# Attention products of a chunk in one TensorE run with a drain, key transposes three chunks ahead, order keys set anew

## The chip, the cores and the metric

The kernel runs on one core of one Trainium2 chip. The metric is device time in microseconds of a whole execution. The kernel before takes 573.67 us, the median of three runs that lie between 573.64 and 573.75.

## The reference

An attention block with a decaying state (4 batches, 8 heads, 768 steps, head size 48) is followed by a feed-forward block over the 3072 tokens (384 in, 2048 hidden).

```python
for t in range(S):
    cur = np.einsum('bhd,bhe->bhde', u[None] * kt, vt)
    y[:, :, t] = np.einsum('bhd,bhde->bhe', rt, state + cur)
    state = wt[:, :, :, None] * state + np.einsum('bhd,bhe->bhde', kt, vt)
...
h = x @ w_in
g = h * np.clip(h + 3.0, 0.0, 6.0) / 6.0
return g @ w_out
```

## The kernel before

**Tiling.** The 768 steps of a batch are cut into chunks of 128, so there are 24 chunks, numbered 0 to 23; neighbouring numbers belong to two different batches, so that a chunk's state comes from the chunk two numbers before. A chunk is worked on as two halves of 64 steps. Eight heads lie as four pairs, one head of a pair on partitions 0 to 47, the other on 64 to 111. Four chunks make a block of 512 tokens, and the feed-forward part runs over six blocks. Block 0 uses plain products (`up`, L639; half of `down`, L658); every other product of the feed-forward part uses seven half-size products in place of eight (`up_product`, L740; `down_product`, L791). All matrices are fp32; on TensorE each matmul stands in the trace as two records.

**One chunk.** `back_scan` (L372, VectorE) runs over the decays from the end and gives E, `make_k` (L392) multiplies the keys with it, `fore_scan` (L381) and `make_r` (L396) do the same for the receptance. From chunk 7 on the two multiplications are GpSimd's. `own` and `own_dot` or `own_sum` give the diagonal of the score matrix, `diagonal` (L431, ScalarE) writes it into A with eight instructions, `above` (L447, VectorE) lays the upper triangle of the scores over it. TensorE has five parts: `score` (L440, 16 matmuls of 48 rows), `turn_k` (L456, four transposes of the keys over the full array), `write` (L536, up to 16 matmuls of 64 rows: keys times values, what the chunk adds to the state), `read_state` (L514, up to 16 matmuls of 48 rows: the state's share of the output) and `read_values` (L523, 16 matmuls of 64 rows: A times values). The last two add into the same PSUM tile y_ps from different rows of the array. `turned_k`, `written` and `leave` (ScalarE, L461, L543, L606) copy results out of PSUM.

**Two runs on TensorE.** From chunk 4 on, `begin(i)` issues `read_state(i)` and the transposes of chunk i+2; `read(i)`, later, issues `write(i+2)`, `read_values(i)` and `score(i+1)`. Feed-forward products stand between the two. For the last two chunks there is no `write`, and `read` issues a TensorE drain before `read_values` (L560). Chunks 0 to 3 use `read_last` and `read_rest` (L566 to L590), which have drains of their own and in which three chosen rows of a fourth pair go through an extra product (L584). Keys are transposed on their own (`turn`) up to chunk 5.

**Buffers.** K has two buffers, W (which becomes R) two, E, kn, kvs and the PSUM tiles y_ps and ps one each. The loads of a chunk's features (feat_in, 676 KB) share three buffers with 22 loads by which the kernel examines its inputs again (`refetch`, L820): a feature buffer comes free when the chunk's K and R (and `own` up to chunk 8) are made.

**Order.** `Plan` (L83 to L185) sets the order of all instructions when the program is built. Each step is added with an engine, an assumed duration, the steps that it needs, the rings of buffers that it holds and a key. The planner walks through an assumed time and, on the engine that can start first, takes the ready step with the lowest key. It emits matmuls of an identity on TensorE (`spin`, L1130) where it expects idle time before the first step of `up`. The keys come from the constants in L28 to L39: LAG and LEAD say how far ahead of its place in a block a chunk's `read` and `begin` are due, AHEAD when features are made, START the features of the first six chunks, CONV the conversion of the weights from 64-bit words (L331 to L359), UP the first block's up products, SUMS the sums of weights for the seven-product form (L687 to L712).

Of the kernel before, what the change touches and what calls it, by code (L numbers as in the profile page):

```python
# [23 lines left out]
BC = 4  # L24
GBC = 3


LAG = 6.1  # L28
AHEAD = -3.5
LEAD = 2.5  # L30
BEHIND = (-1, -1, -1, 0, 6, 7)
BY_PE = 9
OWN = 0.07
SOLO = (0, 2, 3, 4, 5)
EARLY = 7
START = (-118.3, -135.2, -24.4, -60.3, -5.9, 13.2)
CONV = (-100.6, 7.2)
UP = (-68.7, 1.2, -9.3, 6.3)
SUMS = (52.1, 1.4)  # L39
LEAST = 2.0 ** -60  # L40
# [147 lines left out]
def fast_path(tc, feat, tok, wflat, ub, ug, moe_w_in, moe_w_out, out, flag, n_chunks):  # L188
# [21 lines left out]
    with ExitStack() as ctx:  # L210
# [151 lines left out]

        for r, k in (("E", 1), ("K", 2), ("W", 2), ("rk", 1), ("dg", 2), ("A", 2), ("kn", 1), ("S", 2), ("x", 2), ("kvs", 1), ("y", 1),
                     ("ps", 1), ("bankA", 2), ("bankB", 1), ("bankC", 2), ("clip", 2), ("g0", 1), ("g1", 1), ("o", 2),
                     ("T_", 1), ("S_", 1)):
            plan.ring(r, k)
# [22 lines left out]
        def make_k(i):  # L389
            d = st[i]  # L390
            d["K"] = wk.tile([PR, 2 * P, HL], F32, name="K", bufs=2)
            early(i).tensor_mul(d["K"], d["k"], d["E"][:, :, 1:])  # L392
# [59 lines left out]
        def turn_k(i):  # L452
            d = st[i]
            d["kn_ps"] = pp.tile([L, P, PR], F32, name="ps")
            for p in range(P):
                nc.tensor.transpose(d["kn_ps"][:, p, :], d["K"][:, 2 * p:2 * p + 2, :].rearrange("q a t -> q (a t)"), ident[0:PR, 0:PR])  # L456
# [92 lines left out]

        def begin(i):  # L550
            new_y(i)
            read_state(i, range(P))
            if i + 2 < NT:
                turn_k(i + 2)

        def read(i):
            if i + 2 < NT:
                write(i + 2)
            else:
                nc.tensor.drain()  # L560
            read_values(i, range(P))
            if i + 1 < NT:
                score(i + 1)

# [323 lines left out]
        def turned_by(i):  # L888
            return f"turn{i}" if i <= BC + 1 else f"begin{i - 2}"

# [3 lines left out]
        for i in range(NT):  # L894
            t = when(i)
            k = START[i] if i < len(START) else when(i - 2) - AHEAD
            first, last = is_first(i), is_last(i)
            dve = i < EARLY
            behind = [f"fetch{BEHIND[i]}"] if i < len(BEHIND) and BEHIND[i] >= 0 else []
            plan.add(f"feat{i}", "SP", 0.45 if i else 1.15, do(load_feat, i), behind + [f"feat{i - 1}"] * (i > 0) + ["later"] * (i == 1), k - 20, kb=690 if i else 231,  # L900
                     hold=[("feat", [f"K{i}", f"R{i}"] + [f"own{i}"] * (i < BY_PE))])
# [13 lines left out]
            plan.add(f"least{i}", "ACT", 0.2, do(least, i), [f"back{i}"], k + 0.2)  # L915
            if i < BY_PE:
# [15 lines left out]
            plan.add(f"above{i}", "DVE", 0.76, do(above, i), [scored(i), f"diag1{i}"], due + 0.5)  # L932
            if i <= BC + 1:
                plan.add(f"turn{i}", "PE", 0.45, do(turn_k, i), [f"K{i}"] + [f"turn{i - 1}"] * (i > 0), due + 0.01, [("ps", [f"turned{i}"])])
            plan.add(f"turned{i}", "ACT", 0.53, do(turned_k, i), [turned_by(i)] + [f"turned{i - 1}"] * (i > 0), due - 2 if i > BC + 1 else due + 0.5,
                     [("kn", [written_by(i)])])
# [4 lines left out]
            S_ = [("S", [f"read{i}" if i < BC else f"begin{i}"] + [f"state{i}"] * (not last))]  # L941
            if not first:
# [13 lines left out]
            if bk == 0:  # L956
                plan.add(f"first{i}", "PE", 0.55 if first else 0.65, do(read_last, i), [f"above{i}", f"decb{i}"], t + 0.01, y)
                plan.add(f"third{i}", "ACT", 0.5, do(leave_last, i), [f"first{i}"], t + 0.01,
                         ([("x", all_up), ("S_", [f"read{j}" for j in range(BC)])] if i == 0 else []))
                plan.add(f"read{i}", "PE", 2.3 if first else 2.5, do(read_rest, i), [f"third{i}"] + [f"turned{i + 1}", f"tok{i + 1}"] * (i + 1 not in SOLO), t + 0.01)  # L960
                plan.add(f"leave{i}", "ACT", 1.0, do(leave_rest, i), [f"read{i}"], t + 0.02)
            else:
                uses = [f"up{bk}.{q}.{k_}" for q in range(HF) for k_ in (1, 2, 3, 4, 7)] + [f"tx{bk}.1"]
                space = [("x", uses)] * (c == 0)
                needs, us, banks = [f"begin{i}", f"above{i}"], 0.6, []
                if i + 2 < NT:
                    y.append(("ps", [f"turned{i + 2}"]))
                    needs += [f"turned{i + 2}", f"tok{i + 2}"]
                    us += 0.43
                if i + 1 < NT:  # L970
                    needs.append(f"R{i + 1}")
                    banks = [("bankB", [f"above{i + 1}"]), ("bankC", [f"above{i + 1}"])]
                    us += 0.49
                plan.add(f"begin{i}", "PE", 1.04 if i + 2 < NT else 0.6, do(begin, i), [f"decb{i}"] + [f"K{i + 2}"] * (i + 2 < NT),
                         t - LEAD, y)
                plan.add(f"read{i}", "PE", us, do(read, i), needs, t + 0.01, banks)
                plan.add(f"leave{i}", "ACT", 1.5, do(leave, i), [f"read{i}"], t + 0.5, space)
                if c % 2:
                    for g in range(2):
                        plan.add(f"move{bk}.{c // 2}.{g}", "SP", 1.8, do(last_pair, bk, c - 1, c + 1, g, nc.sync),  # L980
                                 [f"leave{i - 1}", f"leave{i}"], when(i) - 50, kb=1, dmas=3)
# [488 lines left out]
```

## Time and profile before

| | |
|---|---|
| median of three runs | 573.67 us (573.64 to 573.75) |
| span of the profiled execution | 570.5 us |
| outside the span, median less span | 3.2 us |
| TensorE matmul busy | 558.8 us, 98% |
| TensorE weight load busy | 501.8 us, 88% |
| VectorE busy | 405.2 us, 71% |
| ScalarE busy | 273.5 us, 48% |
| GpSimd busy | 100.3 us, 18% |
| mean granted TensorE clock | 0.992 |
| first `up` product starts | 32.32 us after the span's start |

The profile shows one execution, whose first and last instruction lie 570.5 us apart. No separate run time of that execution is given; the 3.2 us between its span and the median of the runs is taken as what lies around the span. A timeline row gives start and duration of a group of equal instructions; since matmuls overlap, the time that a group costs is the start of the next group less its own start. Idle time before an instruction stands in brackets with what ended it.

### The profile page before, as it was taken

How to read it: one execution, taken by the hardware profiler on the slowest of the kernel's cores; microseconds unless marked ns; L12 is line 12 of the kernel's file. 1: busy time of each engine (PE TensorE's matmuls, PEld its weight loads, DVE VectorE, ACT ScalarE, POOL GpSimd, SP SyncE). 2: the span in 40 equal slices, each digit the busy share in tenths (PEclk: the TensorE clock that was granted, in tenths of full speed). 3: DMA queues.
4: the chain of work that ended last, by engine and by line, in shares of the span. 5: the costliest groups of instructions: out<-in, count | busy, mean ns of one | idle time of the engine just before them, and what ended most of it. 6: DMA issues, size and time to landing. Idle time of an engine off the chain costs nothing.

```text
span 570.5 us, 13575 instructions
## 1 busy us (share of the span) xinstructions
PE 558.8 (98%) x5636; PEld 501.8 (88%) x5636; DVE 405.2 (71%) x713; ACT 273.5 (48%) x724; POOL 100.3 (18%) x111
## 2 busy tenths in 40 slices
PE   8999899999999999999999999999999999999996
PEld 8898587689888999988999988999988999988996
DVE  7989989988687858767879767879656625255350
ACT  4778664642565633276633366633266611355100
POOL 2000000245513321223123133123122000000000
PEclk9989899999999999999999999999999999999999
DMA  8977822531613236830368360366100001000001
GB/s 279 310 237 223 275 66 63 158 111 42 182 56 90 87 124 204 241 100 9 125 206 274 98 167 7 128 199 225 41 16 2 9 1 36 29 1 1 1 15 47
DMA packets 23078, 63.98 MB, mean 112 GB/s; under 512 B 3120, under 2 KB 10352, under 8 KB 23008
## 3 DMA queue, kind: packets, MB, share of 16 engines
q1 hardware_dynamic: 22880, 63.02, 36.0%
q8 instruction: 46, 0.75, 0.6%
q14 instruction: 24, 0.20, 0.1%
q10 hardware_dynamic: 128, 0.00, 0.0%
HBM read 57.31 MB, written 4.72 MB: 109 GB/s over the span
## 4 chain that ended last, share of the span: by engine, by line
PE 94%; DVE 2%; DMA 1%; ACT 1%; issue 1%; SPq 0%; DVEq 0%; ACTq 0%
PE bankA L791 20%; PE bankA L740 18%; PE bankC L791 10%; PE bankC L740 9%; PE bankB L740 6%; PE bankB L791 5%; PE bankC L639 3%; PE bankA L639 3%; PE bankA L658 3%; PE y_ps L514 3%; PE y_ps L523 2%; PE y_ps L536 2%; PE ps L456 2%; PE bankB L440 2%; DMA feat_in<-in_feat_dram 1%; PE bankA L1130 1%
## 5 line engine op out<-in xcount | busy, mean ns | idle before, releaser
L749 ACT COPY g<-bankA 128x256 f32<-128x256 f32 x120 | 44.3, 371 | 58.7 <-PE bankA L740 56.6
L791 PE MATMUL bankA<-w_out,g 128*128 128x192 f32 x352 | 63.9, 328 | 0.0
L629 ACT ACTIVATE clip<-g,three 128x512 f32<-128x512 f32 x80 | 57.9, 723 | 7.9 <-DVE g L751 7.2
L740 PE MATMUL bankA<-xT,w_in 128*128 128x256 f32 x240 | 60.2, 383 | 0.0
L791 PEld LDWEIGHTS bankA<-w_out,g 128*128 128x128 f32 x352 | 57.9, 190 | 0.9
L759 DVE SCALAR_TENSOR_TENSOR g<-clip,g 128x512 f32<-128x512 f32 x80 | 56.4, 707 | 2.8 <-ACT clip L629 2.6
L804 ACT ACTIVATE o<-bankA 128x192 f32<-128x192 f32 x33 | 10.9, 330 | 88.8 <-PE bankA L791 88.8
L740 PEld LDWEIGHTS bankA<-xT,w_in 128*128 128x128 f32 x240 | 44.8, 190 | 6.0
L431 ACT ACTIVATE A<-eyes,dg 128x64 f32<-128x64 f32 x192 | 49.2, 336 | 0.4
L606 ACT COPY xT<-y_ps 48x256 f32<-48x256 f32 x80 | 29.3, 366 | 37.3 <-PE y_ps L523 36.4
L392 POOL TENSOR_TENSOR K<-feat_in,E 112x512 f32<-112x512 f32 x17 | 21.5, 1266 | 136.6 <-PE bankC L440 121.6
L740 PE MATMUL bankB<-xT,w_in 128*128 128x256 f32 x160 | 41.1, 379 | 0.0
L751 DVE TENSOR_TENSOR g<-bankB,g 128x256 f32<-128x256 f32 x40 | 16.9, 423 | 32.4 <-PE bankB L740 30.7
L396 POOL TENSOR_TENSOR W<-feat_in,W 112x512 f32<-112x512 f32 x17 | 23.1, 1356 | 87.2 <-DVE W L381 87.2
L751 DVE TENSOR_TENSOR g<-bankC,g 128x256 f32<-128x256 f32 x40 | 16.8, 421 | 28.3 <-PE bankC L740 28.2
L740 PEld LDWEIGHTS bankB<-xT,w_in 128*128 128x128 f32 x160 | 30.4, 190 | 4.1
L381 DVE TENSOR_TENSOR_SCAN W<-feat_in,start 112x520 f32<-112x520 f32 x24 | 30.6, 1274 | 3.1 <-PE y_ps L514 3.0
L372 DVE TENSOR_TENSOR_SCAN E<-feat_in,back 112x520 f32<-112x520 f32 x24 | 30.0, 1250 | 2.5 <-DMA feat_in<-in_feat_dram 2.4
L791 PE MATMUL bankA<-bits,g 128*128 128x192 f32 x176 | 30.3, 328 | 0.4 <-DVE o L806 0.4
L791 PE MATMUL bankB<-w_out,g 128*128 128x192 f32 x176 | 30.4, 326 | 0.0
L791 PEld LDWEIGHTS bankA<-bits,g 128*128 128x128 f32 x176 | 28.8, 190 | 0.9 <-DVE o L806 0.7
L791 PEld LDWEIGHTS bankB<-w_out,g 128*128 128x128 f32 x176 | 28.9, 190 | 0.0
(277 smaller groups left out, 1213.8 us busy)
## 6 DMA issues: line engine op xcount, KB each, us to landing
feat_in<-in_feat_dram SPq DMA_DIRECT2D x23, 675.9 KB, 5.6
bits<-in_moe_w_in_dram SPq DMA_DIRECT2D x8, 768.0 KB, 9.6
bits<-in_moe_w_out_dram SPq DMA_DIRECT2D x8, 768.0 KB, 4.7
feat_in<-in_moe_w_in_dram SPq DMA_DIRECT2D x8, 768.0 KB, 4.3
feat_in<-in_moe_w_out_dram SPq DMA_DIRECT2D x8, 768.0 KB, 4.2
rk_in<-in_tok_dram SPq DMA_DIRECT2D x15, 384.0 KB, 5.9
v_in<-in_tok_dram SPq DMA_DIRECT2D x24, 192.0 KB, 4.0
out_dram<-o SPq DMA_DIRECT2D x24, 192.0 KB, 2.1
```

The lines of the kernel that those rows point to most:

```text
L372: nc.vector.tensor_tensor_scan(out=E_[:, ::-1], data0=d["w"][:, :0:-1], data1=back.rearrange("q p t -> q (p t)")[:, ::-1], initial=0.0, op ...
L381: nc.vector.tensor_tensor_scan(out=W_, data0=d["w"][:, :-1], data1=starts[i % 2].rearrange("q p t -> q (p t)"), initial=0.0, op0=ALU.mult, ...
L396: early(i).tensor_mul(d["R"], d["r"], d["R"])
L431: nc.scalar.activation(out=d["A"][:, h, :], in_=eyes, func=ACT.Copy, scale=d["dg"][:, h])
L606: nc.scalar.copy(out=blocks[bk]["xT"][g * GP:g * GP + D, :, at:at + HL], in_=st[i]["y_ps"][(g ^ a) * GP:(g ^ a) * GP + D, a, :, :])
L629: nc.scalar.activation(out=c[:, :m], in_=src, func=ACT.Relu, bias=three, scale=1.0)
L639: nc.tensor.matmul(h_ps[:, :(c1 - c0) * L], lhsT=w_in[:, f // 2, j, f % 2, :], rhs=b["xT"][:, j, c0 * L:c1 * L], start=(j == 0), stop=(j = ...
L740: nc.tensor.matmul(b["p", q, to][:, :HB], lhsT=w, rhs=rhs, start=(n == 0 and k in (1, 2, 5)), stop=(n == len(terms) - 1 and k in (2, 3, 4) ...
L749: nc.scalar.copy(out=to, in_=src)
L751: nc.vector.tensor_add(to, src, to)
L759: nc.vector.scalar_tensor_tensor(out=g, in0=b["r", q, p], scalar=6.0, in1=g, op0=ALU.min, op1=ALU.mult)
L791: nc.tensor.matmul(b["d", p, to][:, :h], lhsT=a, rhs=w(), start=(f == 0 and k in (1, 2, 5)), stop=(f == HF - 1 and k in (2, 3, 4)), skip_g ...
```

## The change

The two runs of a chunk become one. `begin` goes; `read(i)` now issues the transposes of chunk i+3, `read_state(i)`, `score(i+1)`, a drain, `write(i+2)` and `read_values(i)`. The transposes move from two chunks ahead to three, K gets a third buffer, transposes on their own go on to chunk 6, and the features for K (load, `back_scan`, `make_k`, `least`) get keys of their own that are earlier than those of `fore_scan` and `make_r`. The assumed durations of `read` and all keys are new. A parameter of the program's builder sets the scratch space of dynamic DMAs to 8192. What is computed is the same.

```diff
-LAG = 6.1
-AHEAD = -3.5
-LEAD = 2.5
+LAG = 21.433
+AHEAD = -20.818
+AHEAD_K = 3
+EARLIER = 35.468
...
-OWN = 0.07
+OWN = 0.713
...
-START = (-118.3, -135.2, -24.4, -60.3, -5.9, 13.2)
-CONV = (-100.6, 7.2)
-UP = (-68.7, 1.2, -9.3, 6.3)
-SUMS = (52.1, 1.4)
+START = (-107.75, -155.5, -31.0, -50.26, 12.19, 17.64)
+CONV = (-101.07, 9.16)
+UP = (-49.32, 1.47, -3.81, 4.04)
+SUMS = (139.7, -3.91)
...
-            d["K"] = wk.tile([PR, 2 * P, HL], F32, name="K", bufs=2)
+            d["K"] = wk.tile([PR, 2 * P, HL], F32, name="K", bufs=3)
...
-        def begin(i):
+        def read(i):
+            if i + AHEAD_K < NT:
+                turn_k(i + AHEAD_K)
             new_y(i)
             read_state(i, range(P))
-            if i + 2 < NT:
-                turn_k(i + 2)
-
-        def read(i):
+            if i + 1 < NT:
+                score(i + 1)
+            nc.tensor.drain()
             if i + 2 < NT:
                 write(i + 2)
-            else:
-                nc.tensor.drain()
             read_values(i, range(P))
-            if i + 1 < NT:
-                score(i + 1)
...
             k = START[i] if i < len(START) else when(i - 2) - AHEAD
+            kk = k if i < len(START) else when(max(BC, i - AHEAD_K)) - (EARLIER if i > BC + AHEAD_K else EARLIER + 2.0 * (BC + AHEAD_K - i))
...
-            plan.add(f"back{i}", "DVE", 1.4, do(back_scan, i), [f"feat{i}"] + [f"fore{i - 2}"] * (i > 1) + [f"back{i - 1}"] * (i > 0), k,
+            plan.add(f"back{i}", "DVE", 1.4, do(back_scan, i), [f"feat{i}"] + [f"fore{i - 2}"] * (i > 1) + [f"back{i - 1}"] * (i > 0), kk,
...
-                     k + 0.1, [("K", [scored(i), turned_by(i)])], port=True)
+                     kk + 0.1, [("K", [scored(i), turned_by(i)])], port=True)
...
-                     [("W", [scored(i), f"read{i}" if i < BC else f"begin{i}"])], port=True)
+                     [("W", [scored(i), f"read{i}"])], port=True)
...
-                needs, us, banks = [f"begin{i}", f"above{i}"], 0.6, []
+                needs, us, banks = [f"above{i}", f"decb{i}"], 1.15, []
+                if i + AHEAD_K < NT:
+                    y.append(("ps", [f"turned{i + AHEAD_K}"]))
+                    needs.append(f"K{i + AHEAD_K}")
+                    us += 0.4
                 if i + 2 < NT:
-                    y.append(("ps", [f"turned{i + 2}"]))
                     needs += [f"turned{i + 2}", f"tok{i + 2}"]
                     us += 0.43
                 if i + 1 < NT:
                     needs.append(f"R{i + 1}")
                     banks = [("bankB", [f"above{i + 1}"]), ("bankC", [f"above{i + 1}"])]
-                    us += 0.49
-                plan.add(f"begin{i}", "PE", 1.04 if i + 2 < NT else 0.6, do(begin, i), [f"decb{i}"] + [f"K{i + 2}"] * (i + 2 < NT),
-                         t - LEAD, y)
-                plan.add(f"read{i}", "PE", us, do(read, i), needs, t + 0.01, banks)
+                    us += 0.44
+                plan.add(f"read{i}", "PE", us, do(read, i), needs, t + 0.01, y + banks)
...
-    nc = _bacc.Bacc("TRN2", target_bir_lowering=False, num_devices=1)
+    nc = _bacc.Bacc("TRN2", target_bir_lowering=False, num_devices=1, dynamic_dma_scratch_size=8192)
```

In the built program the order of every engine is new. TensorE has the same matmuls apart from 49 identity matmuls instead of 53; the runs of small-array matmuls (`score`, `write`, `read_state`, `read_values`, several in one run if nothing else lies between) are 36 instead of 55.

More of the change, by code (lines that the diff above doesn't have):

```diff
@@ L360, in high_low @@
                                     in1=c["more"].bitcast(I32), op=ALU.add)
-        for r, k in (("E", 1), ("K", 2), ("W", 2), ("rk", 1), ("dg", 2), ("A", 2), ("kn", 1), ("S", 2), ("x", 2), ("kvs", 1), ("y", 1),
+        for r, k in (("E", 1), ("K", 3), ("W", 2), ("rk", 1), ("dg", 2), ("A", 2), ("kn", 1), ("S", 2), ("x", 2), ("kvs", 1), ("y", 1),
                      ("ps", 1), ("bankA", 2), ("bankB", 1), ("bankC", 2), ("clip", 2), ("g0", 1), ("g1", 1), ("o", 2),
@@ L888, in turned_by @@
         def turned_by(i):
-            return f"turn{i}" if i <= BC + 1 else f"begin{i - 2}"
+            return f"turn{i}" if i < BC + AHEAD_K else f"read{i - AHEAD_K}"
         def written_by(i):
@@ L899, in fast_path @@
             behind = [f"fetch{BEHIND[i]}"] if i < len(BEHIND) and BEHIND[i] >= 0 else []
-            plan.add(f"feat{i}", "SP", 0.45 if i else 1.15, do(load_feat, i), behind + [f"feat{i - 1}"] * (i > 0) + ["later"] * (i == 1), k - 20, kb=690 if i else 231,
+            plan.add(f"feat{i}", "SP", 0.45 if i else 1.15, do(load_feat, i), behind + [f"feat{i - 1}"] * (i > 0) + ["later"] * (i == 1), kk - 20, kb=690 if i else 231,
                      hold=[("feat", [f"K{i}", f"R{i}"] + [f"own{i}"] * (i < BY_PE))])
@@ L906, in fast_path @@
                          hold=[("rk_in", [f"own{i}"])])
[L907 removed]
+            plan.add(f"back{i}", "DVE", 1.4, do(back_scan, i), [f"feat{i}"] + [f"fore{i - 2}"] * (i > 1) + [f"back{i - 1}"] * (i > 0), kk,
                      [("E", [f"K{i}", f"least{i}"])], port=True)
             plan.add(f"K{i}", "DVE" if dve else "POOL", 0.66 if dve else 1.32, do(make_k, i), [f"back{i}", f"least{i}"] + [f"K{i - 1}"] * (i > 0) + ["later"] * (i == 0),
[L910 removed]
+                     kk + 0.1, [("K", [scored(i), turned_by(i)])], port=True)
             plan.add(f"fore{i}", "DVE", 1.23, do(fore_scan, i), [f"back{i}"] + [f"fore{i - 1}"] * (i > 0), k + 0.2,
[L912 removed]
+                     [("W", [scored(i), f"read{i}"])], port=True)
             plan.add(f"R{i}", "DVE" if dve else "POOL", 0.66 if dve else 1.32, do(make_r, i), [f"fore{i}"], k + 0.3,
                      port=True)
[L915 removed]
+            plan.add(f"least{i}", "ACT", 0.2, do(least, i), [f"back{i}"], kk + 0.2)
             if i < BY_PE:
@@ L932, in fast_path @@
             plan.add(f"above{i}", "DVE", 0.76, do(above, i), [scored(i), f"diag1{i}"], due + 0.5)
-            if i <= BC + 1:
+            if i < BC + AHEAD_K:
                 plan.add(f"turn{i}", "PE", 0.45, do(turn_k, i), [f"K{i}"] + [f"turn{i - 1}"] * (i > 0), due + 0.01, [("ps", [f"turned{i}"])])
-            plan.add(f"turned{i}", "ACT", 0.53, do(turned_k, i), [turned_by(i)] + [f"turned{i - 1}"] * (i > 0), due - 2 if i > BC + 1 else due + 0.5,
+            plan.add(f"turned{i}", "ACT", 0.53, do(turned_k, i), [turned_by(i)] + [f"turned{i - 1}"] * (i > 0), due - 2 if i >= BC + AHEAD_K else due + 0.5,
                      [("kn", [written_by(i)])])
@@ L940, in fast_path @@
                      [("kvs", [f"decb{i}"] if last else [f"state{i}"])])
-            S_ = [("S", [f"read{i}" if i < BC else f"begin{i}"] + [f"state{i}"] * (not last))]
+            S_ = [("S", [f"read{i}"] + [f"state{i}"] * (not last))]
             if not first:
```

## The prediction

> **What bounds the kernel now.** I read the page's busy line and its clock row, the chain that ended last, TensorE's own waits, then timelines around single chunks. The page first:
>
> ```profile
> PE 558.8 (98%) x5636; PEld 501.8 (88%) x5636; DVE 405.2 (71%) x713; ACT 273.5 (48%) x724; POOL 100.3 (18%) x111
> ...
> PEclk9989899999999999999999999999999999999999
> ...
> PE 94%; DVE 2%; DMA 1%; ACT 1%; issue 1%; SPq 0%; DVEq 0%; ACTq 0%
> ```
>
> TensorE (PE) is busy 98% and is 94% of the chain: time is saved only by issuing less on it, by switching its array less often, or where it stands still or runs at a lower clock. The list of waits, TensorE's alone, shows where it stands still; all of them lie before 151 us:
>
> ```profile
> PE y_ps L536 <- ACT kn L461: 1.6, 2, 0.9
> PE y_ps L584 <- ACT xT L576: 0.6, 1, 0.6
> PE bankB L440 <- DVE A L447: 0.5, 1, 0.5
> PE bankA L658 <- DVE w_out L359: 0.4, 1, 0.4
> ```
>
> The busy table by stretch shows two stretches with half the clock (column PEclk, after five pairs of busy time and count):
>
> ```profile
> 28.90:32.30 3.40, 3.40 (x24) 3.37 (x17) 3.37 (x6) 3.12 (x8) 0.00 (x0) 0.50 0.76 212
> 66.40:69.85 3.45, 3.34 (x17) 1.43 (x20) 3.28 (x4) 2.22 (x5) 0.00 (x0) 0.51 0.92 327
> ```
>
> Each costs 1.7 us (half of 3.4) where TensorE is what counts. The third thing is the switching. A steady chunk in the timeline, first `begin` (L514, L456), then `read` (L536 to L791):
>
> ```profile
> 281.07 1.47 PE L791 MATMUL bankA<-w_out,g 128*128 128x192 f32 x8
> 282.47 0.67 PE L514 MATMUL y_ps<-W,S 48*48 48x64 f32 x32
> 283.06 0.60 PE L456 MATMUL ps<-ident,K 112*128 112x112 f32 x4
> 283.50 1.48 PE L791 MATMUL bankA<-w_out,g 128*128 128x192 f32 x8
> 284.82 2.76 PE L791 MATMUL bankB<-w_out,g 128*128 128x192 f32 x16
> 287.42 1.46 PE L791 MATMUL bankA<-w_out,g 128*128 128x192 f32 x8
> 288.81 0.62 PE L536 MATMUL y_ps<-v_in,kn 64*64 64x48 f32 x30
> ...
> 290.33 1.57 PE L791 MATMUL bankC<-bits,S__3062 128*128 128x192 f32 x8
> 291.74 0.49 PE L791 MATMUL bankB<-w_out,g 128*128 128x192 f32 x2
> ```
>
> Eight L791 records take 1.30 us start to start in full flow (284.82 to 287.42 is 2.60 for 16). The eight ahead of L514 take 1.40 and those ahead of L536 1.39, so entering small tiles costs 0.095. The eight after `read` take 1.41: leaving costs 0.11 there, besides some 0.13 inside the 1.52 of `read` (288.81 to 290.33). `begin` is 0.10 + 0.59 + 0.44 + 0.02 (1.32 for the eight after it) = 1.15 us, `read` 0.09 + 1.52 + 0.11 = 1.72, a chunk 2.87.
>
> What a drain costs shows at chunk 22, which has no keys to turn and nothing to write:
>
> ```profile
> 454.12 0.67 PE L514 MATMUL y_ps<-W,S 48*48 48x64 f32 x32
> 454.90 0.67 PE L523 MATMUL y_ps<-A,v_in 64*48 64x64 f32 x32
> ```
>
> L514 and the gap take 0.78; L514's own starts span 0.45 (0.59 above less the 0.14 to the first transpose). The gap is 0.33, against some 0.03 between small matmuls without a drain.
>
> **What the Trainium skill says.** "TensorEngine Tiling (Array Packing)", section Key Properties, says that a change of tiling mode, not of the tile alone, drains TensorE. The trace agrees: 0.095 us going in and 0.24 coming out, but next to nothing between L536, L523 and L440, whose starts even interleave. "TensorE: Matmul & The Clock Gate", Part 1, says that the clock is halved after an idle window of about 3.4 us and that the windows run free of the kernel; here the two half-clock stretches last 3.41 us, both after stretches full of short matmuls, drains and waits. The same page, Part 3, has weight loads overlap running matmuls only where row groups differ; that a drain forbids even this fits the 0.33.
>
> **The change part by part.**
>
> *One run instead of two* (18 chunks, 4 to 21). Transposes between full-size products take 0.39 us (startup, L456 at 44.87, next product at 45.26). So the new run is: transposes 0.39 and 0.02, entry 0.095, L514 0.45, L440 with L536 and L523 and the way out 1.52 + 0.11, the drain 0.30 more than a plain step, and 0.03 because L440 now follows L514 and no longer slides into L523 (that overlap was -0.025, the step from L440 to L514 at 62.2 us is 0.038). Sum 2.92 against 2.87: +0.05 a chunk, +0.9 us in all. One entry and one exit go (0.095 + 0.24), a drain comes (0.30), and the transposes lose a place where they covered part of the exit. Bounds: drain gaps in the startup are 0.305 to 0.35 and the L440 overlap may stay, so 0.00 to +0.11 a chunk, 0 to +2.0 us. Chunk 22 keeps its one drain; chunk 23 had two runs with a drain in the second and gets one, -0.2. Together **+0.7**, from -0.2 to +1.8. The drain queues `write(i+2)`, `read_values(i)` and the products after them, nothing else.
>
> *Startup, the new order.* Four identity matmuls less (0.28 each) count only as far as nothing else is late. I followed the new order of the engines with the durations of the rows. `own` of chunk 0 moves behind K and R, so the scores come 0.6 us earlier; ScalarE then has the copy of kvs for chunk 0 ahead of the second half of the diagonal, and the first two chunks leave at about the old time. Before, the last copy of chunk 1 ended at 30.27, yet the first up product started at 32.32, behind six identity matmuls at half clock. Now four stand there, and the dot of another chunk has moved away: start at about 30.7. If the half clock stays until 32.3, 0.8 of those 1.6 us is left. After that VectorE has three conversions of weights ahead of the first gate (three times 2.4 us), ready about 36.8, and TensorE needs that gate at 37.3: no wait, but no margin either. The waits of L440 (0.5) and of L658 (0.4) should go: all 16 first-half up products now stand ahead of the first down product, and the scores of chunks 2 and 3 are apart. Down products now stand between `read_last` and L584 of chunks 2 and 3, which covers the 0.6 us, and they should fill the stretch whose emptiness precedes the second half clock, 1.7. Full sum 0.8 + 0.5 + 0.4 + 0.6 + 1.7 = 4.0. What my walk gives at the end of chunk 3, with the four down records less that before had not got to counted at 0.644 us per matmul, is 3.3; I take **-3.3**, bounds -4.5 and -0.8 (half clock again, gate late).
>
> *Chunks 4 to 8.* The two waits for kn (1.6) should go, kn being made a chunk earlier. In their place the new order has two `own_dot` in a row, the second waiting for VectorE's `own` of the next chunk (one buffer rk): some 1.4, and 0.2 at a bank of the scores. VectorE was busy 46.2 of 50 us from 50 to 100 us and must now have done a further back scan (1.25) by each point, so this is where it can bind. **0**, from -1.2 to +1.5.
>
> *Feature loads.* K of a chunk is made earlier, R not: on GpSimd K of chunk 9 now stands ahead of R of chunk 7. A feature buffer is held two chunks longer, all three are taken most of the time, and the refetches share them. A load now comes nearer to its back scan, which stands at VectorE's head: gate steps and PSUM reads of feed-forward products queue behind it, and TensorE waits for those. Loads land in 5.6 us (median); before, the scans waited 2.4 us in all, and nothing passed on. I take **+0.3**, from 0 to +3. What of SP is moved (value loads, output stores) keeps several us.
>
> *Third K buffer, scratch setting, new sums of weights:* 0; memory only, or VectorE work beside the 6 to 20 idle us per 50 us that it has from 100 us on.
>
> Sum: 0.7 - 3.3 + 0 + 0.3 = -2.3 us. The span goes from 570.5 to 568.2; with 3.2 us around it as before, 571.4 us.
>
> **The rivals.** *No gain:* the walk is too rosy. If the second half clock stays (+1.7) and the first gate is late by another 0.6, the startup gives 1.0, the run costs 0.7, the loads 0.3: 573.7. For it: the page's VectorE row is at 8 to 9 tenths there; against: the new order puts dense down products into the empty stretch. *Cheaper run:* drain and overlap at their best and startup at its full 4.0, kn's wait half gone: 573.67 - 4.0 - 0.2 - 0.6 = 568.9. For it: the exit of 0.24 is certain to go; against: all three must hold. *Slower, late features:* with the buffers held longer, a load is issued only when R of two chunks back is done, and lands after VectorE has come to the scan. A product's bank is needed again after about 1.3 us, of which an eviction takes 0.4, so TensorE has some 0.6 to spare; a scan that waits 1.6 us costs it 1.0. At seven of the 15 later loads that is 7 us, less 2.6 gained: 578; at five, 576. It decides against the change from three such scans on, when VectorE's idle time for feature loads passes some 8 us in place of 2.4. Against it: VectorE's key for the loads is 35 us ahead.
>
> **How the numbers follow.** A measurement here tells 0.2%, 1.15 us, from no change. Forecast 571.4: chance 0.50 (of it 0.43 faster by more than that, 0.06 within, 0.01 slower). No gain, 573.7: 0.20 (0.02, 0.15, 0.03). Cheaper run, 568.9: 0.13, all faster. Late features, 576: 0.17 (0.01 within, 0.16 slower). Faster 0.58, same 0.22, slower 0.20. The range, 568.6 to 575.6, reaches into the cheaper run and into the weaker half of the late features. The cases that are faster hold most of the chance; theirs alone is 568.6 to 572.5.
>
> **What would show it.** A steady run of one chunk of 2.85 to 3.0 us with a gap of 0.3 ahead of L537; the first up product before 31.5; one half-clock stretch instead of two; no TensorE wait for kn, but one of 1 to 1.5 at L416; VectorE idle for feature loads under 4 us. A drain gap under 0.2 or over 0.45, a later start of the up products, or TensorE waits after 150 us would make it wrong.

## The result and the profile after

The changed kernel takes 576.83 us (median of 20 runs, 575.01 to 580.81); the kernel before, run beside it, takes 573.20 (20 runs, 571.01 to 580.74). The ratio is 1.0068 with an interval of 1.0048 to 1.0089: 3.9 us slower. The prediction was 571.4, with a range up to 575.6: the sign is wrong, and the time lies outside the range. The profiled execution took 575.67 us with a span of 573.9. A few executions of a kernel (7 of 222 of the kernel before, further down) take over 1.5% longer than its fastest one; ratios leave them out.

One correction of my own baseline first. Every run lists its span beside its time, and in runs of both kernels they differ by 1.7 to 1.8 us. The profiled execution of before, with a span of 570.5, must have taken 572.3, not 573.67; the 3.2 us "around it" were 1.4 too many. In spans, I forecast -2.3 us and the profiles show +3.4. Of these, 2.5 lie ahead of the start of the last product; the other 0.9 lie behind it, where two profiles of the order of before differ as much (5.6 and 6.5 us).

The page of the kernel after, the same rows as before:

```profile
PE 555.9 (97%) x5628; PEld 503.0 (88%) x5628; DVE 411.4 (72%) x713; ACT 272.4 (47%) x724; POOL 107.3 (19%) x111
...
PEclk9999999999999999999999999999999999999999
...
PE 81%; DVE 1%; issue 1%; DMA 1%; SPq 0%; ACT 0%; DVEq 0%
```

TensorE is less busy in a longer span: it waits more. (Its share of the chain can't be compared with the 94% of before: here the chain is followed back only to 80.8 us, and the shares add up to 84%.) VectorE and GpSimd (POOL) do the same number of instructions in 6 and 7 us more. TensorE's waits:

```profile
PE y_ps L537 <- issue: 2.5, 15, 0.2
PE bankC L637 <- DVE g L648: 1.8, 1, 1.8
PE ps L416 <- DVE rk L406: 1.6, 1, 1.6
...
PE bankC L637 <- DVE A L448: 0.9, 1, 0.9
```

The waits of before (kn, xT, A at L440, w_out) are gone, and three longer ones stand in their place; the first row is the drain (15 of 20; the others stand under other releasers).

Where the time went, from the starts of the matmuls in each trace: I counted every matmul begun by a given time at its undisturbed start-to-start step (L738 216 ns, L789 163, L656 323, transposes 111, dots 112, small tiles 17; identity matmuls at nothing), and took the sum from the elapsed time. What is left is waiting, switching and draining, and the loss to half clock, which is read off the granted clock microsecond by microsecond and taken off too. "Again" is a second profile of the order of before (eighth experiment).

| stretch, us | before | again | after |
|---|---|---|---|
| 0 to 75 | 24.5 | 25.4 | 25.0 |
| 75 to 104 | 1.8 | 1.8 | 3.6 |
| 104 to 150 | 2.5 | 2.9 | 1.4 |
| 150 to 300 | 2.6 | 2.2 | 4.5 |
| 300 to 460 | 2.1 | 2.1 | 4.1 |
| 460 to the last product | 0.9 | 0.9 | 0.1 |
| sum | 34.4 | 35.3 | 38.7 |
| taken off for half clock | 3.4 | 1.7 | 1.7 |

The startup gains nothing; 75 to 104 us loses 1.8; 104 to 150 us wins 1.1 (the second wait for kn, at 150 us, is gone); from 150 to 460 us some 4 are lost. Of these, 0.8 comes back behind 460 us, where before still has the runs of its last chunk to do (at 468 and 471 us; after, the last run starts at 458). In what is left, 3.1, stalls of over 0.1 us between large products, at 210, 294, 357 and 402 us, are 1.8 (start to start, so more than the idle time that the rows show); the run is 0.08 in each of 13 chunks, 1.0; one more chunk lies in this stretch than before, 0.3.

### The profile page after: what moved, and what is told of

Same layout as the page of the kernel before. It is cut to its first block, busy times and chain, and to the rows that moved or that the text cites. A ratio compares the mean times of both kernels' runs of the same rounds, so it can differ in the third digit from the quotient of the medians.

```text
span 573.9 us, 13581 instructions
## 1 busy us (share of the span) xinstructions
PE 555.9 (97%) x5628; PEld 503.0 (88%) x5628; DVE 411.4 (72%) x713; ACT 272.4 (47%) x724; POOL 107.3 (19%) x111
## 4 chain that ended last, share of the span: by engine, by line
PE 81%; DVE 1%; issue 1%; DMA 1%; SPq 0%; ACT 0%; DVEq 0%
PE bankA L789 20%; PE bankA L738 18%; PE bankC L789 10%; PE bankC L738 9%; PE bankB L738 6%; PE bankB L789 5%; PE bankA L656 2%; PE y_ps L537 2%; PE y_ps L515 2%; PE y_ps L524 2%; PE bankA L637 1%; PE bankB L441 1%; PE ps L457 1%; DMA feat_in<-in_feat_dram 1%; PE bankC L637 1%
## 5 line engine op out<-in xcount | busy, mean ns | idle before, releaser
L789 PE MATMUL bankA<-w_out,g 128*128 128x192 f32 x352 | 62.5, 328 | 0.4 <-ACT o L802 0.4
L757 DVE SCALAR_TENSOR_TENSOR g<-clip,g 128x512 f32<-128x512 f32 x80 | 60.1, 755 | 3.7 <-ACT clip L627 3.7
L738 PE MATMUL bankA<-xT,w_in 128*128 128x256 f32 x240 | 60.6, 381 | 0.0
L789 PEld LDWEIGHTS bankA<-w_out,g 128*128 128x128 f32 x352 | 58.1, 190 | 1.6 <-ACT o L802 0.7
L393 POOL TENSOR_TENSOR K<-feat_in,E 112x512 f32<-112x512 f32 x17 | 26.1, 1533 | 147.4 <-DVE E L373 136.8
L738 PEld LDWEIGHTS bankA<-xT,w_in 128*128 128x128 f32 x240 | 45.2, 190 | 5.9
L738 PE MATMUL bankB<-xT,w_in 128*128 128x256 f32 x160 | 41.1, 379 | 0.0
L738 PEld LDWEIGHTS bankB<-xT,w_in 128*128 128x128 f32 x160 | 30.4, 190 | 4.0
L789 PE MATMUL bankA<-bits,g 128*128 128x192 f32 x176 | 31.1, 329 | 0.0
L789 PE MATMUL bankB<-w_out,g 128*128 128x192 f32 x176 | 30.6, 326 | 0.0
L789 PEld LDWEIGHTS bankA<-bits,g 128*128 128x128 f32 x176 | 28.7, 190 | 0.4
L789 PEld LDWEIGHTS bankB<-w_out,g 128*128 128x128 f32 x176 | 28.9, 190 | 0.0
```

The lines of the kernel that those rows point to most:

```text
L738: nc.tensor.matmul(b["p", q, to][:, :HB], lhsT=w, rhs=rhs, start=(n == 0 and k in (1, 2, 5)), stop=(n == len(terms) - 1 and k in (2, 3, 4) ...
L757: nc.vector.scalar_tensor_tensor(out=g, in0=b["r", q, p], scalar=6.0, in1=g, op0=ALU.min, op1=ALU.mult)
L789: nc.tensor.matmul(b["d", p, to][:, :h], lhsT=a, rhs=w(), start=(f == 0 and k in (1, 2, 5)), stop=(f == HF - 1 and k in (2, 3, 4)), skip_g ...
```

## The experiments

Many of them only move a step: the planner's order is left alone, and then a named step is put ahead of another (`own6` is `own` of chunk 6, `back7` the key scan of chunk 7, `shift5`, `join5`, `full5` the VectorE steps of the fifth conversion counted from nought). "Less half clock" is the median of each run's time less (1 - mean granted clock) times its span. All ratios are to the kernel before, run beside the kernel in question; they are not the quotients of the medians in the table (for the fifteenth that would be 1.0019). "Faster than after" compares medians of runs made at different times; the median of before moved between 573.1 and 573.8 in them, and an interval is some 1.1 us wide on either side, so a difference of 1 us says little.

| kernel | us | ratio, interval | less half clock |
|---|---|---|---|
| before (222 runs over all) | 573.45 | 1 | 568.3 |
| after | 576.83 | 1.0068, 1.0048 to 1.0089 | 573.3 |
| 2: two rk buffers | 574.98 | 1.0037, 1.0018 to 1.0056 | 572.2 |
| 13: rk ahead of the scan | 574.99 | 1.0032, 1.0019 to 1.0045 | 571.5 |
| 15: gates first | 574.55 | 1.0005, 0.9986 to 1.0025 | 571.0 |
| 16: scores first | 574.79 | 1.0022, 1.0003 to 1.0040 | 570.6 |
| 6: gates and scores | 573.19 | 0.9990, 0.9963 to 1.0016 | 571.1 |
| 7: moves, dot later | 574.16 | 0.9994, 0.9974 to 1.0014 | 570.9 |
| 11: moves without the dot | 571.48 | 0.9963, 0.9942 to 0.9985 | 568.0 |
| 14: all moves | 571.79 | 0.9977, 0.9963 to 0.9990 | 568.0 |
| 8: before, three K buffers | 572.88 | 0.9983, 0.9959 to 1.0006 | 568.3 |
| 12: before, kn earlier | 571.08 | 0.9960, 0.9939 to 0.9980 | 567.4 |
| 9: rows paired, no drain | 570.50 | 0.9943, 0.9921 to 0.9965 | 566.3 |
| 10: rows paired, drain | 578.05 | 1.0065, 1.0035 to 1.0095 | 572.4 |

### Does the half clock belong to the order? (8)

```diff
-d["K"] = wk.tile([PR, 2 * P, HL], F32, name="K", bufs=2)
+d["K"] = wk.tile([PR, 2 * P, HL], F32, name="K", bufs=3)
-nc = _bacc.Bacc("TRN2", target_bir_lowering=False, num_devices=1)
+nc = _bacc.Bacc("TRN2", target_bir_lowering=False, num_devices=1, dynamic_dma_scratch_size=8192)
```

> The kernel before, order untouched, with the third K buffer and the scratch setting of the changed kernel. Both theories: no difference, 573.1 within 0.8. It gives a second profile of the order of before: if the half-clock stretches of the profile shown (28.9 and 66.4 us) belong to that order, they lie at the same times again; if they fall where the throttle happens to count, they lie elsewhere, and the 2.5 us that I had the change gain by them were not its to gain.

No difference in time, as expected. The stretches of this profile, and then that of the kernel after (PEclk is the third figure from the end):

```profile
28.90:32.30 3.40, 3.29 (x45) 3.04 (x45) 3.23 (x6) 3.32 (x10) 0.00 (x0) 1.00 0.88 269
64.40:67.80 3.40, 3.29 (x51) 2.13 (x49) 3.23 (x5) 2.63 (x5) 0.00 (x0) 0.54 0.74 224
```

```profile
98.60:102.05 3.45, 3.45 (x8) 2.04 (x8) 3.35 (x9) 2.18 (x9) 0.00 (x0) 0.51 0.91 243
```

In the same order of instructions the first half-clock stretch, 28.9 to 32.3 us, isn't there, and the first up product starts at 31.5 us instead of 32.3. The second comes again, 2 us earlier. In the twelfth experiment, whose startup is that of before, both are there, each twice as long (6.8 us). So the first comes in some executions, the second in all three profiles. The kernel after has neither, but one of its own: between 94 and 108 us in 11 of the 13 profiles taken of its order with and without small edits. Earlier ones come in its order too: at 38 us in two of the 13 (fifth, tenth), at 11 to 12 us in three (fifth, seventh, fifteenth). Over all runs the median granted clock is 0.991 before and 0.9935 after, 5.1 and 3.7 us of half-clock loss: 1.4 us for the change. I had booked 1.7, for the second stretch going away. (The 2.5 of the expectation adds the 0.8 of an earlier start inside the first stretch; but there the prediction had the half clock stay.)

### The waits in the new order, one at a time (15, 16, 2, 13)

```diff
+('K3', 'up0.4.0'), ('shift5', 'up0.4.0'), ('join5', 'up0.4.0'), ('full5', 'up0.4.0')
```

> The changed kernel with one move alone: the first two gates and K of chunk 3 ahead of the fifth conversion of weights. TensorE's wait for the gate was 1.8 us: 575.0 if it is time of the kernel; no difference if the fifth conversion, now 1.5 us later, is waited for instead.

The gate and the product that waits for its bank, in the kernel after:

```profile
37.19 0.41 DVE L648 SCALAR_TENSOR_TENSOR g<-clip,bankC 128x256 f32<-128x256 f32 x1
...
37.66 1.56 PE L637 MATMUL bankC<-xT,w_in 128*128 128x256 f32 x6 [1.84 <-DVE g L648]
```

and with the gates ahead of the fifth conversion:

```profile
35.99 0.41 DVE L648 SCALAR_TENSOR_TENSOR g<-clip,bankC 128x256 f32<-128x256 f32 x1
...
36.95 1.56 PE L637 MATMUL bankC<-xT,w_in 128*128 128x256 f32 x6
```

No idle time stands ahead of the product, and the kernel is 2.3 us faster, with and without the half clock: the wait was its time.

```diff
+('back7', 'up0.8.2'), ('least7', 'up0.8.2'), ('K7', 'up0.8.2')
```

> The changed kernel with one move alone: the key scan of chunk 7, and so GpSimd's product of it, behind the state and scores of chunk 4. TensorE's wait of 0.9 us for A goes, and VectorE's product of the state there takes 0.36 us in place of 1.23, since GpSimd no longer works beside it: 575.9. If the later scan makes the key transposes of chunk 7 late: no difference.

In the kernel after:

```profile
83.30 1.36 POOL L393 TENSOR_TENSOR K<-feat_in,E 112x512 f32<-112x512 f32 x1 [79.28 <-DVE E L373]
83.65 1.23 DVE L470 TENSOR_TENSOR S<-S,w_min 112x192 f32<-112x192 f32 x1
...
85.61 1.56 PE L637 MATMUL bankC<-xT,w_in 128*128 128x256 f32 x6 [0.93 <-DVE A L448]
```

and with the move:

```profile
81.38 0.36 DVE L470 TENSOR_TENSOR S<-S,w_min 112x192 f32<-112x192 f32 x1
...
83.77 1.47 PE L637 MATMUL bankC<-xT,w_in 128*128 128x256 f32 x6
...
84.03 1.18 POOL L393 TENSOR_TENSOR K<-feat_in,E 112x512 f32<-112x512 f32 x1 [80.02 <-PE ps L457]
...
84.33 1.10 DVE L486 TENSOR_TENSOR state<-S,kvs 112x192 f32<-112x192 f32 x1
```

VectorE's small product of the state takes 0.36 us alone and 1.23 beside GpSimd's product of K; in the moved order the slow one is the state sum (1.10), for which nobody waits. The Trainium skill, "SBUF — State Buffer", section "SBUF: two separate sides", says that the port pair of VectorE and GpSimd is an exclusive lock, which a VectorE operation with two SBUF inputs needs when the GpSimd operation reads SBUF; these lines agree: each slow operation ends 0.2 us after GpSimd's. The wait of 0.9 us is gone and the kernel 2.0 us faster (2.7 without the half clock). That is more than the wait; where the rest comes from isn't shown.

```diff
-d["rk"] = wk.tile([PR, P, L], F32, name="rk", bufs=1)
+d["rk"] = wk.tile([PR, P, L], F32, name="rk", bufs=2)
```

(the same for the other rk tile)

> The changed kernel with two buffers for rk instead of one, order untouched, so that VectorE can form rk of chunk 6 before TensorE has read rk of chunk 5. My theory (the new keys put two dots in a row and TensorE waits 1.6 us for the second, and VectorE stands too): the wait of L416 goes, 1.0 to 1.7 us less, and some 1.3 more in executions where the half-clock stretch that follows at 98.6 us goes with it: 574 to 575.5. Rival (the time comes back at the next wait, since VectorE is what is late in this stretch): within 0.5 us of the changed kernel.

1.9 us faster (1.1 without the half clock; the interval overlaps that of the kernel after), but a wait of 0.6 stayed, since a scan stands ahead of rk on VectorE. With `('own6', 'back8')` besides:

> The changed kernel with two rk buffers and, on VectorE, rk of chunk 6 ahead of the key scan of chunk 8. In the second experiment two buffers alone left a wait of 0.6 us, and in the eleventh one of 1.3, since VectorE has a scan of 1.24 us ahead of that product. If the wait of 1.6 us is time of the kernel: it goes whole, 576.8 becomes 575.2 or less (less still where the half-clock stretch behind it goes too). If the scan that now comes later makes the next chunk's keys late: within 0.6.

The kernel after, and then this one:

```profile
96.09 1.37 DVE L406 TENSOR_TENSOR rk<-feat_in 112x512 f32<-112x512 f32 x1 [0.24 <-PE ps L416]
...
97.60 1.02 PE L416 MATMUL ps<-u_col,rk 112*128 112x2 f32 x8 [1.56 <-DVE rk L406]
```

```profile
94.03 0.69 DVE L406 TENSOR_TENSOR rk<-feat_in 112x512 f32<-112x512 f32 x1
...
95.98 1.05 PE L416 MATMUL ps<-u_col,rk 112*128 112x2 f32 x8 [0.25 <-ACT dg L422]
```

1.8 us faster: no more than with the buffers alone, or 0.7 more without the half clock. In the kernel after, rk itself is one of the slow products beside GpSimd (1.37 us, 0.69 here).

### Moves together (6, 7, 11, 14)

The sixth has the moves of 15 without K3, and those of 16.

> The changed kernel with two moves in its order: on VectorE the first two gates stand ahead of the fifth conversion of weights rather than behind it, and the scan of the keys of chunk 7 (with its product on GpSimd) stands behind the state and scores of chunk 4 rather than ahead of them. If TensorE's waits of 1.8 us (first gate) and 0.9 us (A) are time of the kernel: 2.7 us less, 574.1. If VectorE is what is late in the startup, so that the next conversion or gate makes TensorE wait in their place: within 0.8 us of the changed kernel.

3.6 us faster than after (2.2 without the half clock). TensorE waited 1.4 us for K of chunk 3 in the gate's place: K stood behind the conversion that was pushed back.

```diff
+('dot6', 'gate0.10.2'), ('state15', 'refetch10'), ('back23', 'least23')
```

The seventh has these besides, and two rk buffers.

> The changed kernel with the two moves of the sixth experiment, two rk buffers and the second of the two dots one down product later, and at 293 and 401 us the state sum and the key scan behind the gate sums that TensorE waits for. If the waits add up: 1.8 + 0.9 + 1.6 + 0.9 = 5.2 us less, 571.6, faster than the kernel before. If half of each comes back elsewhere: 574.

Too high an expectation: with the dot behind a down product, that product came forward and waited 1.9 us for its weights. Leaving the dot where it was, and putting K3 ahead too:

> The changed kernel with the moves of the sixth experiment, K of chunk 3 also ahead of the fifth conversion, two rk buffers (the dots stay where they are), and the two moves at 293 and 401 us. In the sixth, TensorE waited 1.4 us for K of chunk 3, 1.2 for rk, 0.6 for a gate sum; in the seventh 1.9 us for weights since a down product came forward. If these are time of the kernel: 2 us under the sixth (573.2), so 571 to 572, and faster than the kernel before by 1 to 2. If the startup is bound by VectorE's sum of work: as the sixth.

571.48, 5.3 us faster than after, with and without the half clock, and 0.4% faster than before. With rk ahead of the scan as well:

> The eleventh experiment (571.5) with rk of chunk 6 ahead of the key scan as well. If the 1.3 us that TensorE waited there are time of the kernel: 570.2. If not: 571.5 within 0.6.

571.79: 1.0 of the dot's wait of 1.3 us is gone, and the time is not less; TensorE waited 0.6 us for down weights there instead. Alone the moves are worth 2.3, 2.0 and 1.8 us, together 5.0 to 5.3: with an uncertainty of some 1 us each, this doesn't show whether they add up.

Where they won it, by the count of the table above: up to 104 us the kernel after loses 28.6 us, the eleventh 25.8 and the fourteenth 25.3. From 150 to 460 us it is 8.6 after, 8.6 and 8.1 here, 7.1 in the seventh, and 4.7 before. So the moves took away waits ahead of 104 us; of what is lost behind 150 us these two kernels gave back next to nothing. The two moves meant for that stretch have to be read one by one.

The move at 401 us did what it was to do. In the kernel after, a gate sum (0.69 us beside an idle GpSimd) is stretched, and the product after it is late:

```profile
400.46 1.19 POOL L393 TENSOR_TENSOR K<-feat_in,E 112x512 f32<-112x512 f32 x1 [4.36 <-DVE E L373]
400.64 1.54 DVE L774 TENSOR_TENSOR S__4420<-g,S__4420 128x512 f32<-128x512 f32 x1
...
402.33 1.54 PE L789 MATMUL bankC<-w_out,S__4420 128*128 128x192 f32 x8 [0.43 <-ACT o L802]
```

(The row names ScalarE's copy, but the operand S is ready only at 402.2.) With the scan behind the sum (fourteenth), that product follows without idle time:

```profile
397.37 0.69 DVE L774 TENSOR_TENSOR S__4420<-g,S__4420 128x512 f32<-128x512 f32 x1 [1.47 <-PE bankA L789]
397.98 1.23 DVE L373 TENSOR_TENSOR_SCAN E<-feat_in,back 112x520 f32<-112x520 f32 x1
...
398.47 1.46 PE L789 MATMUL bankC<-w_out,S__4420 128*128 128x192 f32 x8
```

The stall at 294 us stayed, 0.4 start to start in the kernel after and 0.8 in the fourteenth. It begins with a feature load. In the kernel after:

```profile
285.92 1.24 DVE L373 TENSOR_TENSOR_SCAN E<-feat_in,back 112x520 f32<-112x520 f32 x1 [1.16 <-DMA feat_in<-in_feat_dram]
...
294.52 1.57 PE L789 MATMUL bankA<-bits,S__3190 128*128 128x192 f32 x8 [0.26 <-DVE S__3190 L774]
```

The scan waits 1.16 us for the load, VectorE is busy from there to the sum that the product needs, and TensorE stands still for 0.26. In ten profiles with this order of steps (after, 1, 2, 5, 6, 9, 10, 13, 15, 16) the scan's wait runs from 0.75 to 2.24 us, and TensorE's idle time at this product is that wait less 0.9 us each time (0.88 to 0.90): none for 0.75, 0.26 for 1.16, 0.69 for 1.58, 1.35 for 2.24. With the move at 293 us it is the wait less 1.42 (0.06 for 1.48 in the seventh, 0.58 for 2.01 in the eleventh, 0.62 for 2.04 in the fourteenth). So the move did win 0.5 us of slack; the loads landed later in the profiles of the eleventh and fourteenth, and earlier in that of the seventh. The kernel before has one such wait behind 150 us (0.76 and 1.03 us in its two profiles), and nothing comes of it.

### What the drain costs (1, 5, 9, 10)

State products and values reach the same output rows from different array rows, and the drain orders them. These kernels change the rows, at the same number of matmuls, so that no drain is needed; what they put out for chunks 4 to 23 is not what the reference puts out.

```diff
-rows = slice(g * GP, g * GP + D)
+h = a if i >= BC else g
+rows = slice(h * GP, h * GP + D)
...
-**into(i, a, p, g))
+**into(i, a, p, h))
...
-nc.tensor.drain()
```

> The changed kernel, except that in chunks 4 to 23 the second half of the state products (L515) is issued on the array rows and output rows of the first half, so that the same number of matmuls runs but no drain is needed ahead of the writes, and the drain is left out; the output of those chunks is not the reference's. No instruction moves. If a drain costs what its gap shows (score to kv 0.384 us where a plain step takes some 0.03, so 0.35 in each of 20 chunks), the time falls by 7.0 us, from 576.8 to about 569.8. If products after the run make good for the drain (their banks and gates being late anyway), it falls by less than 4. If the loss of the change lies in the run alone, this kernel would also be faster than the kernel before (573.2) by about 3.

578.14: not faster. The gap went, but the 32 state products, two after another on a row group and all with the same output rows, took 0.92 us instead of 0.45.

```diff
-for a in range(is_first(i), 2):
-    for g in range(2):
+for a, g in ([(a, a) for _ in range(2) for a in range(is_first(i), 2)] if i >= BC else ...):
```

> As the first experiment, but the state products of chunks 4 to 23 (all on the output rows of the first half, output not the reference's) take the two row groups of the array in turn, so that they overlap as in the changed kernel; the drain is left out. In the first experiment the drain's gap of 0.38 us went, but state products on one row group took 0.92 us for 32 instead of 0.45, which ate it up. If that was all: the run of a chunk falls from 2.93 to 2.55 us, in 20 chunks 7 us, 576.8 to about 570. If what comes after the run waits anyway: a fall of under 3 us.

578.56: a miss again. In turn on two row groups, with the same output rows, they took 0.88 us:

```profile
219.67 1.04 PE L515 MATMUL y_ps<-W,S 48*48 48x64 f32 x30
220.51 0.27 PE L441 MATMUL bankB<-W,K 48*64 48x64 f32 x1
...
220.55 0.22 PE L515 MATMUL y_ps<-W,S 48*48 48x64 f32 x2
```

```diff
-half = slice(a * HL, (a + 1) * HL)
+half = slice((g if i >= BC else a) * HL, ((g if i >= BC else a) + 1) * HL)
```

(values; in the writes of chunks 6 on, `g ^ a` in place of `a`)

> The changed kernel, in which the values (L524, chunks 4 to 23) and the writes (L537, chunks 6 to 23) read the other half of their tokens where that puts them on the array rows that the state products use for the same output rows; the output of those chunks is not the reference's. The number of matmuls and the overlap of array rows and output rows stay as they were; no drain is needed, and it is left out. If the drain costs what its gap shows and nothing hides it: a chunk's run of 2.93 us falls by 0.35 to 0.38, in 20 chunks 7.0 to 7.6 us against the same kernel with its drain. If the products after it wait in its place: under 3 us.

> The same as the ninth experiment with the drain kept: the control for it. Both theories: as the changed kernel, 576.8 within 1, a chunk's run of 2.9 to 2.95 us; the difference of the two is the price of 20 drains.

570.50 without, 578.05 with the drain: 7.55 us for 20 drains, 0.38 each, as much as its gap in the trace (6.1 us and 0.30 without the half clock, of which the tenth had more; the two intervals leave some 2 us of doubt). So little or nothing hides it. The tenth is 1.2 us above the kernel after, and 0.9 below it without the half clock. A steady chunk, in the kernel after (rows left out at the dots):

```profile
214.38 0.55 PE L457 MATMUL ps<-ident,K 112*128 112x112 f32 x4
214.86 0.67 PE L515 MATMUL y_ps<-W,S 48*48 48x64 f32 x32
...
215.77 0.22 PE L441 MATMUL bankC<-W,K 48*64 48x64 f32 x1
216.15 0.62 PE L537 MATMUL y_ps<-v_in,kn 64*64 64x48 f32 x30 [0.17 <-issue]
...
217.21 1.57 PE L789 MATMUL bankA<-bits,g 128*128 128x192 f32 x8
```

and in the ninth experiment:

```profile
212.72 0.22 PE L441 MATMUL bankC<-W,K 48*64 48x64 f32 x1
212.75 0.58 PE L537 MATMUL y_ps<-v_in,kn 64*64 64x48 f32 x30
...
213.77 1.41 PE L789 MATMUL bankA<-bits,g 128*128 128x192 f32 x7
```

From the last score to the first write it is 0.38 us with the drain and 0.03 without. Step by step, a chunk is 2.93 us after, 2.855 before and 2.54 without a drain: one run saves 0.31, and the drain that it needs takes 0.39.

### Half of the change each (3, 4)

> The new run of the changed kernel with the order keys of the kernel before (LAG, AHEAD, START, CONV, UP, SUMS, OWN as before, the scan of the keys placed by the same offset as before, one chunk earlier). If the run itself costs what I read in the trace (2.93 us a chunk against 2.855, so 1.4 in 18 chunks, 0.45 less in chunks 22 and 23) and the keys cost the rest: 0 to 1.5 us over the kernel before, 573 to 574.7. If the run is what costs the 3.9 us (what queues behind its drain), 576 to 578.

597.12 us, ratio 1.0392 (1.0350 to 1.0434).

> The two runs of the kernel before (begin and read, key transposes two chunks ahead) with the order keys of the changed kernel, three K buffers and its scratch setting. If the keys cost the time (waits for the first gate, for A and for the second dot before 100 us): 575 to 577, about 1 us under the changed kernel. If the run is what costs it: 572 to 573.5, as the kernel before.

581.47 us, ratio 1.0128 (1.0097 to 1.0158). Both missed both expectations. The planner places everything anew when a step or a key changes; in the third kernel TensorE waited 6 us for K and kn, and the median loss to half clock is 12.8 us; in the fourth it stood 5.2 us for one eviction. Crossed like this, they measure neither the run nor the keys. I took the price of the run from the steady chunks and the ninth and tenth runs instead.

### The kernel before, with its waits for kn removed (12)

```diff
+('down0.0.7', 'diag05'), ('turn5', 'down0.0.7'), ('turned5', 'down0.0.7'),
+('turned10', 'read8'), ('down0.1.4.1', 'read8'), ('out0.1.c21', 'read8'), ('store0.3', 'read8')
```

> The kernel before, with its two waits for kn taken away in its own order: the key transposes of chunk 5 one down product earlier and their copy ahead of the diagonal on ScalarE, the first run of chunk 8 one down product earlier. No third K buffer, no drain, no new keys. The waits are 0.9 and 0.7 us of TensorE: 1.6 us less, 571.5 where the kernel before takes 573.1. If the copy that now stands ahead of the diagonal makes the scores late: no difference.

571.08, 0.4% faster than before (0.9 us without the half clock): the waits for kn could be taken away in the old order, by small moves in two places, though one of 1.1 us for rk came. Like the eleventh and the fourteenth, this kernel is faster than both.

## Why the prediction was wrong

*One run instead of two* (+0.7): right in mechanism, too small by 0.5. I took a gap of 0.33 for the drain; it is 0.38. A chunk costs 0.077 us more, not 0.05; with the last two chunks about +1.2.

*Startup, the new order* (-3.3): this step failed. 1.7 of it was the second half-clock stretch. I had cited the Trainium skill, "TensorE: Matmul & The Clock Gate", Part 1, for windows that run free of the kernel, and still took the stretches of one execution as what an order has or has not, and booked none for the new order. Of the two, one comes and goes, and the other moved to 98 us. In the medians 1.4 us less was lost to half clock, near the 1.7, but not as I had it (that "one half-clock stretch instead of two" came true is chance). The other 1.6 did not come at all: by 75 us, without half clock, the count is 25.0 us against 24.5 and 25.4. What failed there is the gate: "ready about 36.8, and TensorE needs that gate at 37.3". TensorE was early, as forecast (first up product at 29.86, forecast 30.7), so it needed the gate at 35.8; the gate ended at 37.6, and the 1.5 us of waits that did go were paid back as one of 1.8.

*Chunks 4 to 8* (0): the waits for kn went (1.6) and the second dot's came (1.6; I had 1.4), both as forecast. The "0.2 at a bank of the scores" was 0.9: I followed VectorE's durations from rows where GpSimd stood idle, and the keys made three chunks ahead bring GpSimd's first product just there.

*Feature loads* (+0.3): this step failed too, since apart from the run it was all that I booked for the time after 150 us, and the stalls there are 1.8; "TensorE waits after 150 us" stands among its own signs of being wrong. The path that it names is real: at 294 us a late load passes through VectorE to TensorE once the scan has waited over 0.9 us. But VectorE's idle time for loads rose only from 2.4 to 4.4 us, not to the 8 of the late-features rival. The other part I had put at nothing: ahead of the stalls at 210, 294, 357 and 402 us the trace shows VectorE's 512-element products at 1.2 to 1.7 us beside GpSimd, where they take 0.7 alone. At 402 us a move shows that this makes the stall; at 210 and 357 us I didn't test it.

*Third K buffer, scratch setting* (0): right (572.88).

The slower rival named 576, near the result; that is luck, since it had 7 us of late scans for it.

What is shown of the cause: with the structure unchanged and every drain in place, five moves and a buffer give back 5.3 us, so the waits ahead of 104 us come from the new keys' order and are time of the kernel. The run is not free either: some 1.2 us of the loss are its own. The stalls behind 150 us come from late loads and from VectorE beside GpSimd where lines or moves show it, and the seventh, whose loads came early and whose order has the two moves, has next to none of them: its 7.1 us behind 150 us are 2.4 above before, of which the run, the chunk more and the end of the last chunk explain 2.1. What stays open is why the half-clock stretch moved to 94 to 108 us: it follows the two dots, but it also came (1.7 us lost) where the second dot's wait was gone (thirteenth and fourteenth), and it was missing twice where a wait of 1.2 to 1.4 us stood (first and sixth).

## What to carry to other kernels

Don't book a half-clock stretch as a gain from one profile: look at several executions of an order, expect the stretch to move, and compare times less their clock loss. When a step is pulled ahead, look at who needs the engine just then and at what runs beside it: a short VectorE product beside GpSimd took three times as long. A load that comes late for one engine costs another nothing until the slack between them is used up, and then all that is over it: compare several executions before you call it harmless. Before two switches are merged into one, price the drain that the merger makes necessary against the switch that it saves.

## What the runs showed of the hardware that I had not expected

In these kernels small matmuls (48 by 48 weights, 64 columns moved) overlapped fully only when the output rows changed too: 32 took 0.45 us over both halves of the output rows, and 0.88 us when the array rows changed from each to the next but the output rows did not. The Trainium skill, "TensorEngine Tiling (Array Packing)", section Key Properties, says that different tiles can run in parallel; here, tiles that share their output rows did not. (In the fifth experiment each output element is also added to twice, two matmuls apart; whether that alone would slow them wasn't tested.)
